# Second layers of seven experts with the token slots stationary, in an attention and expert-routing kernel on one Trainium2 core

## The chip, the cores and the metric

The kernel runs on one core of a Trainium2 chip. The core has engines with instruction streams of their own: TensorE (PE in the profile; its weight loads are listed apart as PEld), VectorE (DVE), ScalarE (ACT), GpSimd (POOL) and SyncE (SP, which here only issues transfers). The metric is the device time of one execution in microseconds (us), lower is better. The kernel before takes 544.92 us (median of 3 runs, 543.99 to 547.03).

## What is computed

Attention over 4 batches, 8 heads, 768 positions, 64 values per head, in which a query sees the first 8 keys and the last 96; the result, 3072 tokens of 512 values, goes into a layer of 8 experts. Each token goes to one expert, the one with the largest gate logit. All arrays are fp32.

```python
def _moe_ref(x, w_gate, w1, w2):          # x: (3072, 512), w1: (8, 512, 1024), w2: (8, 1024, 512)
    logits = x @ w_gate
    expert_idx = np.argmax(logits, axis=1)
    # gate_w: the softmax of logits at expert_idx; tokens sorted by expert (...)
    for e in range(E):
        lo, hi = (boundaries[e], boundaries[e + 1])
        h = np.maximum(x_sorted[lo:hi] @ w1[e], 0.0)
        y_sorted[lo:hi] = h @ w2[e]
    y = y_sorted[inv_perm]
    return gate_w[:, None] * y
```

## The kernel before

The kernel runs attention in units of (batch, pair of heads, third of the sequence), 48 in all. For each unit TensorE makes scores, ScalarE takes exponentials, VectorE multiplies them with the mask and bias, and TensorE multiplies with the values (`attend`). Every second unit is turned (`turn`) so that the gate logits can be made while attention goes on. Finished tokens are stored in `x_tok` in device memory, and an expert's tokens are gathered from there by GpSimd with indices that earlier steps have sorted. Two blocks of expert 0's tokens are looked up and worked on before attention is over; the rest of expert 0 comes as p = 0 in the loop below, with 208 slots.

The experts have fixed numbers of slots, and expert 2 and later are taken in order of their counts:

```python
CAPS = (464, 416, 416, 400, 400, 368, 368, 272)
ORDER = (0, 1, 2, 3, 4, 7, 5, 6)          # so p = 1..7 have 416, 416, 400, 400, 272, 368, 368 slots
NQ = 4
# P = 128, DM = 512, KC = 4, FC = 8, TB = 4, NJ = 4, E = 8
```

The end of attention. `n0` counts units in steps of two, and `nu` is 48:

```python
                for n in two:
                    ...
                    scores(n)
                    ...
                if n0 == nu - 4:
                    fetch_0(0)        # pw = sel x mw on TensorE, rows on VectorE, 8 gathers on GpSimd
                    count_0()         # c2 on TensorE, early on VectorE
                if n0 >= 4:
                    turn(n0 - 4)      # px: four transposes on TensorE, copied by ScalarE
                    for n in two:
                        attend(n - 2)
                ...
                if b == B - 1 and m == 6:
                    half_0(0)         # n0 = 42: makes mw, the operand of pw, on VectorE
    ...
            attend(nu - 2)
            turn_x(xe_0, xq_0[0], TB)                     # VectorE turns gathered rows
            turn(nu - 4)
            attend(nu - 1)
            turn_x(xe_0[:, :, P:2 * P], xq_0[1], TB)
            work(1)                                       # a piece of expert 0's layers on TensorE
            turn(nu - 2)
            expert_w1(w1_1, slice(1, 2))
            work(1)
            logits(B - 1)
            ...
            rows_of(ps_m, "_s", NR * NQ, st.pop(("w", 2)), rows_s)
            identify()
            sort_acc(1, gslot_s)
            fit()
            work(3)
            ...
```

`pw`, `c2`, `px`, `pq` (the logits) and the tables share two PSUM buffers (tag "m").

An expert, cut to what TensorE does and what follows it:

```python
            def sort(p, part, parts):             # VectorE turns part of expert p's gathered rows into xe
                ...
            def hidden(p, between=None):          # first layer: slots move, w1 is stationary
                C = slots(p)
                w1t, xe = ws[p % 2][0], xes.pop(p)
                hT = hp.tile([P, FC, CM], F32, tag="hT", name=f"hT_{p}")
                hTs[p] = hT
                for fc in range(FC):
                    ph = ps_h.tile([P, 512], F32, tag="ph", name=f"ph_{p}_{fc}")
                    for kc in range(KC):
                        nc.tensor.matmul(ph[:, 0:C], lhsT=w1t[:, 0, kc, P * fc:P * fc + P], rhs=xe[:, kc, 0:C],
                                         start=(kc == 0), stop=(kc == KC - 1))
                    done = nc.scalar.activation(hT[:, fc, 0:C], ph[:, 0:C], AF.Relu)
                    if fc < 2 and between:
                        between(2 * fc, 2 * fc + 2)      # the turn of the expert before: two blocks each
                    pace(1 if fc < FC - 1 else len(pending), done)   # gathers of a later expert, held back until done

            def result(p):                        # second layer: slots move, w2 is stationary
                ...
                yT = hp.tile([P, KC, CM], F32, tag="yT", name=f"yT_{p}")
                def turn(q0, q1):                 # back to rows of tokens, 128 at a time
                    for q in range(q0, min(q1, (C + P - 1) // P)):
                        ...
                        for dc in range(KC):
                            nc.tensor.transpose(pt[0:rows, P * dc:P * dc + P], yT[:, dc, o:o + rows], ident)
                        finish(p, q, rows, pt)    # times the gate on VectorE, then a scatter to the output
                cuts = [0, C] if p < E - 1 else [0, (C - 1) // P * P, C]
                for g in range(len(cuts) - 1):
                    c0, c1 = cuts[g:g + 2]
                    for dc in range(KC):
                        po = ps_o.tile([P, DM], F32, tag="po", name=f"po_{p}_{g}_{dc}")
                        for fc in range(FC):
                            nc.tensor.matmul(po[:, 0:c1 - c0], lhsT=w2t[:, 0, fc, P * dc:P * dc + P], rhs=hT[:, fc, c0:c1],
                                             start=(fc == 0), stop=(fc == FC - 1))
                        pace(2 if dc == 0 else 1, nc.vector.tensor_copy(out=yT[:, dc, c0:c1], in_=po[:, 0:c1 - c0]))
                        if p > 0 and 0 < dc < KC - 1:
                            sort(p + 1, dc - 1, KC - 2)
                        ...
                return turn

            for p in range(1, E):
                hidden(p, turn)
                fetch(p + 2, 0)                   # w1 of the expert after next
                plan(p + 2)                       # its gathers
                turn = result(p)
                fetch(p + 2, 1)                   # its w2
```

The early blocks of expert 0 and the gate logits already have the two forms that matter below: `result_0` keeps 128 slots of `hT_0` stationary and moves 512 columns of `w2_0` (`po`, line 340), and `logits` keeps 32 columns of `wg_sb` stationary and writes four groups of 32 partitions (`pq`, line 559).

## Time and profile before

| | |
|---|---|
| time, median of 3 runs | 544.92 us (543.99 to 547.03) |
| span of the profiled execution | 525.5 us |
| granted TensorE clock, mean | 0.993 |
| TensorE's first instruction | at 4.7 us |
| part of the experts' loop (from 197.5 us on) | 328.0 us, TensorE busy 319.9 |
| last TensorE instruction ends | at 517.4 us |

The profile comes from one execution. In it an engine's busy time is the time covered by its instructions, and the chain that ended last is followed back from the last instruction, at each step to what released it or to the instruction before it on its engine. An L and a number name a line of the kernel; `out<-in` are the tensors written and read; a matmul in fp32 shows as two rows. Rows of TensorE overlap[...], so its pace is read from starts, or from the chain, and not from the duration of one.

### The profile page before, as it was taken

What the parts mean: (1) busy time and instruction counts of PE and PEld (TensorE: products, weight loads), DVE (VectorE), ACT (ScalarE), POOL (GpSimd) and SP (SyncE); (2) the same over time, 40 slices, a digit from 0 to 9 for tenths busy, and PEclk for the clock granted to TensorE, in tenths of its full rate; (3) what the DMA queues carried; (4) which work ended last, traced back from release to release, by engine and by line L of the source; (5) the groups of instructions that cost most, each with busy time, mean ns of one, the idle gap of its engine ahead of it and who ended that gap; (6) DMA issues with size and microseconds to landing.
All of it is one profiled execution on the core that took longest, in us unless ns stands there. A gap on an engine that the chain in (4) does not pass through costs nothing.

```text
span 525.5 us, 7951 instructions
## 1 busy us (share of the span) xinstructions
PE 506.7 (96%) x3076; PEld 380.6 (72%) x3076; DVE 197.2 (38%) x506; ACT 126.5 (24%) x227; POOL 136.7 (26%) x161
## 2 busy tenths in 40 slices
PE   4999999999979999999999999999999999999993
PEld 3999999999979949855555556556556886666793
DVE  5877897896954534110320122022012031022011
ACT  4766655654632102011001001101100101101100
POOL 5000000000041276342344226334222735202002
PEclk9999999999989999999999999999999999999998
DMA  9999999899936922954461816456083686001001
GB/s 155 157 155 163 235 164 179 224 164 176 276 113 183 277 54 84 212 181 95 100 217 49 173 40 222 91 107 230 16 175 98 175 172 222 20 1 57 1 2 61
DMA packets 145184, 71.95 MB, mean 137 GB/s; under 512 B 126656, under 2 KB 126660, under 8 KB 145136
## 3 DMA queue, kind: packets, MB, share of 16 engines
q1 hardware_dynamic: 137344, 58.16, 49.0%
q0 software_dynamic: 5264, 12.59, 8.0%
q10 hardware_dynamic: 2528, 0.59, 0.6%
q8 instruction: 26, 0.43, 0.3%
q14 instruction: 22, 0.18, 0.1%
HBM read 59.00 MB, written 12.65 MB: 136 GB/s over the span
## 4 chain that ended last, share of the span: by engine, by line
PE 94%; DVE 2%; POOL 1%; DMA 1%; issue 0%; SPq 0%; ACT 0%; POOLq 0%
PE po L1089 29%; PE ph L1046 29%; PE o L528 14%; PE s L493 8%; PE px L545 3%; PE po L340 3%; PE ph L333 2%; PE pt L1079 2%; PE pq L559 1%; DMA x_tok<-xr 1%; PE pi L618 1%; PE first L428 1%; DVE e L506 0%; DVE kT L429 0%; DVE w_second L510 0%
## 5 line engine op out<-in xcount | busy, mean ns | idle before, releaser
L273 POOL DMA_INDIRECT xq_s<-x_tok,rows_s x72 | 72.6, 1009 | 133.4 <-DVE yT L1091 58.9
L1091 DVE COPY yT<-po 128x416 f32<-128x416 f32 (+6 forms) x36 | 17.6, 488 | 229.4 <-PE po L1089 229.4
L1048 ACT ACTIVATE hT<-ph 128x416 f32<-128x416 f32 (+4 forms) x64 | 29.9, 468 | 281.4 <-PE ph L1046 281.4
L1089 PE MATMUL po<-hT,w_second 128*128 128x416 f32 (+4 forms) x320 | 80.4, 411 | 0.0
L1046 PE MATMUL ph<-xe,w_second 128*128 128x416 f32 (+3 forms) x256 | 80.2, 469 | 0.0
L1046 PE MATMUL ph<-xe,w_first 128*128 128x208 f32 (+3 forms) x256 | 76.5, 456 | 0.0
L1089 PE MATMUL po<-hT,w_first 128*128 128x208 f32 (+3 forms) x256 | 75.5, 456 | 0.0
L1089 PEld LDWEIGHTS po<-hT,w_second 128*128 128x128 f32 x320 | 56.1, 190 | 23.9 <-issue 10.2
L1046 PEld LDWEIGHTS ph<-xe,w_second 128*128 128x128 f32 x256 | 48.0, 190 | 28.1 <-issue 9.9
L1089 PEld LDWEIGHTS po<-hT,w_first 128*128 128x128 f32 x256 | 47.7, 190 | 27.1 <-issue 10.2
L1046 PEld LDWEIGHTS ph<-xe,w_first 128*128 128x128 f32 x256 | 47.3, 190 | 25.8 <-issue 10.0
L273 POOL DMA_INDIRECT xq<-x_tok,rows x15 | 15.3, 1023 | 165.8 <-DVE early L645 142.0
L528 PE MATMUL o<-vt,e 128*128 128x128 f32 x288 | 53.9, 278 | 0.0
L528 PE MATMUL o<-va,e 128*128 128x128 f32 x240 | 46.9, 277 | 0.0
L528 PEld LDWEIGHTS o<-vt,e 128*128 128x128 f32 x288 | 43.2, 195 | 0.2 <-issue 0.2
L493 PE MATMUL s<-qT,kT 64*128 64x128 f32 x384 | 38.7, 286 | 0.9 <-ACT qT L430 0.9
L314 POOL DMA_INDIRECT out_dram<-y,idx_s x21 | 20.5, 976 | 71.8 <-DVE y L322 68.8
L499 ACT ACTIVATE e<-s 128x1024 f32<-128x1024 f32 (+1 forms) x36 | 33.0, 943 | 18.2 <-PE s L493 18.2
L528 PEld LDWEIGHTS o<-va,e 128*128 128x128 f32 x240 | 36.9, 194 | 0.1
L493 PE MATMUL s<-qT,kA 64*128 64x128 f32 x320 | 34.2, 292 | 2.0 <-ACT kA L414 2.0
L493 PEld LDWEIGHTS s<-qT,kT 64*128 64x128 f32 x384 | 30.2, 196 | 2.2 <-ACT qT L430 1.3
L510 DVE TENSOR_TENSOR e<-e,Wb 128x1024 f32<-128x1024 f32 x24 | 28.8, 1213 | 7.4 <-ACT e L499 7.3
(170 smaller groups left out, 491.9 us busy)
## 6 DMA issues: line engine op xcount, KB each, us to landing
w_second<-in_moe_w_dram SPq DMA_DIRECT2D x16, 512.0 KB, 8.6
w_second<-in_moe_w_dram SPq DMA_DIRECT2D x4, 2048.0 KB, 9.1
x_tok<-xr SPq DMA_DIRECT2D x24, 256.0 KB, 3.8
w_first<-in_moe_w_dram SPq DMA_DIRECT2D x12, 512.0 KB, 8.6
w_first<-in_moe_w_dram SPq DMA_DIRECT2D x3, 2048.0 KB, 9.2
vt<-in_v_dram SPq DMA_DIRECT2D x31, 192.0 KB, 3.8
w_second<-in_q_dram SPq DMA_DIRECT2D x60, 96.0 KB, 3.6
w_second<-in_k_dram SPq DMA_DIRECT2D x60, 96.0 KB, 2.9
```

What stands on the lines that cost most here:

```text
L273: return nc.gpsimd.indirect_dma_start(out=xq[:, i, :], out_offset=None, in_=x_tok[0:NJ * top, :], in_offset=bass.IndirectOffsetOnAxis(ap=c ...
L314: p = nc.gpsimd.indirect_dma_start(out=out[:, :], out_offset=bass.IndirectOffsetOnAxis(ap=where, axis=0), in_=y[0:rows, :], in_offset=None ...
L340: nc.tensor.matmul(po, lhsT=hT_0[q][:, fc, :], rhs=w2_0[:, 0, fc, :], start=(fc == 0), stop=(fc == FC - 1))
L493: nc.tensor.matmul(ps[:, h, P * m:P * m + P], lhsT=lhsT, rhs=qT[r, P * i:P * i + P], start=True, stop=True)
L499: nc.scalar.activation(e[:, :, 0:w], ps[:, :, 0:w], AF.Exp, scale=D ** -0.5)
L510: nc.vector.tensor_tensor(out=eh, in0=eh, in1=W[:, 2 * j:2 * j + 2, P:3 * P].rearrange("p h (o c) -> p h o c", o=1).to_broadcast([P, 2, 2, ...
L528: nc.tensor.matmul(po[:, t, h, :], lhsT=pt[:, h, P * m:P * m + P], rhs=(vt if own else va)[:, c0:c0 + P], start=(m == mine[0][0]), stop=(m ...
L545: nc.tensor.transpose(px[:, 2 * i + t, :], xrs[b, c][:, t, P * j:P * j + P], ident)
L1046: nc.tensor.matmul(ph[:, 0:C], lhsT=w1t[:, 0, kc, P * fc:P * fc + P], rhs=xe[:, kc, 0:C], start=(kc == 0), stop=(kc == KC - 1))
L1048: done = nc.scalar.activation(hT[:, fc, 0:C], ph[:, 0:C], AF.Relu)
L1089: nc.tensor.matmul(po[:, 0:c1 - c0], lhsT=w2t[:, 0, fc, P * dc:P * dc + P], rhs=hT[:, fc, c0:c1], start=(fc == 0), stop=(fc == FC - 1))
L1091: pace(2 if dc == 0 else 1, nc.vector.tensor_copy(out=yT[:, dc, c0:c1], in_=po[:, 0:c1 - c0]))
```

## The change

For p = 1 to 7 the second layer is turned round: 128 slots of `hT` are stationary and the 512 columns of `w2` move, so that the result stands in rows of tokens and need not be transposed. What is left beyond full blocks, where it is at most 96 slots, is done in pieces of 32 slots: four column groups of TensorE each take the same 32 slots and 128 columns of `w2`, and the result lies as 128 partitions of (group, slot) x 128 values, which a scatter puts into the output seen as rows of 128. A longer rest (112) is one more block. To scale such a piece the gates are needed in its layout, which `gates_of` makes for all pieces once. A last partial piece is padded with zeros in `hT`. Expert 0 keeps the old form (`along_row`). `hT` has two buffers. The next expert's rows are turned behind the first two blocks. Apart from that, the look-up for expert 0's first blocks moves behind the first `attend` of its step, and `count_0` behind a piece of expert 0's work.

```diff
+    gpc_0 = consts.tile([P, LOTS[1] * TB], F32)
+    gpc_s = consts.tile([P, NR * NQ * TB], F32)
@@
+    def gates_of(pool, ps, nm, ns, gs, to):
+
+        mg = pool.tile([P, NS, TB], F32, tag="mw", name="mg" + nm, bufs=1)[:, 0:ns, :]
+        nc.vector.tensor_tensor(out=mg, in0=gs.rearrange("p (s o) -> p s o", o=1).to_broadcast([P, ns, TB]),
+                                in1=grp.rearrange("p (o g) -> p o g", o=1).to_broadcast([P, ns, TB]), op=ALU.mult)
+        pg = ps.tile([P, NS * TB], F32, tag="m", name="pg" + nm)[:, 0:TB * ns]
+        nc.tensor.matmul(pg, lhsT=sel, rhs=mg.rearrange("p s g -> p (s g)"), start=True, stop=True)
+        nc.vector.tensor_copy(out=to, in_=pg)
@@ (put() takes the view of the output that it writes; scaled() returns its instruction)
+    out_j = out.rearrange("n (j d) -> (n j) d", j=NJ)
@@
-                if n0 == nu - 4:
-                    fetch_0(0)
-                    count_0()
                 if n0 >= 4:
                     turn(n0 - 4)
                     for n in two:
                         attend(n - 2)
+                        if n == nu - 4:
+                            fetch_0(0)
@@
             work(1)
+            count_0()
             turn(nu - 2)
@@
             sort_acc(1, gslot_s)
+            work(1)
+            gates_of(gp, ps_m, "_s", NR * NQ, gslot_s.rearrange("p r q -> p (r q)"), gpc_s)
+            gates_of(gp, ps_m, "_1", LOTS[1], gslot_0[1], gpc_0)
             fit()
-            work(3)
+            work(2)
@@
-            hp = ectx.enter_context(tc.tile_pool(name="hp", bufs=1))
+            hp = ectx.enter_context(tc.tile_pool(name="hp", bufs=2))
@@ (in hidden)
+                if C % 32 > 0:
+                    nc.vector.memset(hT[:, :, C:C // 32 * 32 + 32], 0.0)
@@
+            def finish_piece(p, i, pt):
+
+                r = ORDER[p] - 2
+                c = 2 * TB * p + i if p < 2 else NQ * TB * r + i
+                g, rw = (gpc_0, rows_0[1]) if p < 2 else (gpc_s, rows_s)
+                y = yp.tile([P, DM], F32, tag="y", name=f"y_{p}_p{i}")[:, 0:P]
+                nc.vector.tensor_scalar(out=y, in0=pt, scalar1=g[:, c:c + 1], scalar2=None, op0=ALU.mult)
+                put(y, P, rw[:, c:c + 1], out_j)
@@ (along_row(p, C, w2t, hT) is the old second layer and its turn, without sort() and cuts)
+            def result(p):
+
+                C = slots(p)
+                w2t, hT = ws[p % 2][1], hTs.pop(p)
+                if p == 0:
+                    return along_row(p, C, w2t, hT)
+                rest = C % P if C % P <= 3 * 32 else 0
+                nq = (C - rest + P - 1) // P
+                for q in range(nq):
+                    rows = min(P, C - P * q)
+                    po = ps_o.tile([P, DM], F32, tag="po", name=f"po_{p}_{q}")
+                    for fc in range(FC):
+                        nc.tensor.matmul(po[0:rows, :], lhsT=hT[:, fc, P * q:P * q + rows], rhs=w2t[:, 0, fc, :],
+                                         start=(fc == 0), stop=(fc == FC - 1))
+                    pace(2, finish(p, q, rows, po))
+                    if q < 2:
+                        sort(p + 1, q, 2)
+                for i in range(TB * nq, pieces_of(C) if rest else 0):
+                    pt = ps_t.tile([P, P], F32, tag="pt", name=f"pt_{p}_{i}")
+                    for fc in range(FC):
+                        for g in range(TB):
+                            nc.tensor.matmul(pt[32 * g:32 * g + 32, :], lhsT=hT[:, fc, 32 * i:32 * i + 32],
+                                             rhs=w2t[:, 0, fc, P * g:P * g + P], start=(fc == 0), stop=(fc == FC - 1))
+                    finish_piece(p, i, pt)
```

## The prediction

> **What bounds the kernel.** I read the page first, then the chain that ended last in order of time, then the stretch around 146 us where that chain leaves TensorE. The page's busy times and the chain's shares by engine:
>
> ```profile
> PE 506.7 (96%) x3076; PEld 380.6 (72%) x3076; DVE 197.2 (38%) x506; ACT 126.5 (24%) x227; POOL 136.7 (26%) x161
> ...
> PE 94%; DVE 2%; POOL 1%; DMA 1%; issue 0%; SPq 0%; ACT 0%; POOLq 0%
> ```
>
> TensorE is on the chain for 94% of the span, so a microsecond taken from TensorE's own work is a microsecond off the end, unless another engine then comes late. From the chain in order of time (start, us, what), one stretch of expert 0's early work, one of the gate logits, and then one whole expert of 416 slots with the next one's start:
>
> ```profile
> 168.65 1.48 PE pq L559 x32
> ...
> 185.62 12.05 PE po L340 x28
> ...
> 243.62 22.35 PE po L1089 x64
> 265.97 2.79 PE ph L1046 x8
> 268.76 0.87 PE pt L1079 x8
> 269.63 2.80 PE ph L1046 x8
> 272.43 0.87 PE pt L1079 x8
> ...
> 494.96 15.59 PE po L1089 x80
> ```
>
> Each fp32 matmul is two rows here (8 fc x 4 dc = 32 matmuls, 64 rows); a transpose is one row. What to see: (a) the second layer with 416 slots moving costs 22.35/64 = 349 ns a row; (b) a block's four transposes cost 0.87/2 = 0.437 us, 109 ns each, on the chain between the next expert's first layers; (c) with 512 columns moving and 128 slots stationary (po L340, the form the change uses) a row costs 12.05/28 = 430 ns; (d) with 32 stationary columns and outputs on four partition groups (pq L559) 32 rows of 192 columns take 1.48 us, 46 ns a row. The same chain gives 335.8 ns for 400 slots (21.49/64), 309.2 for 368 (19.79/64), 229.2 for 272 (14.67/64).
>
> Then the timeline around the one long pause of TensorE, and busy time by stretch (us, PE, PEld, DVE, ACT, POOL busy, granted clock, DMA share, GB/s):
>
> ```profile
> 147.61 0.36 PE L268 MATMUL pw<-mw,sel 128*128 128x8 f32 x2 [1.29 <-DVE gslot L633]
> 147.82 0.37 PE L644 MATMUL c<-C_b,ones 128*128 128x8 f32 x2
> 149.80 1.11 PE L545 MATMUL px<-ident,xr 128*128 128x128 f32 x4 [1.61 <-DVE early L645]
> ```
>
> ```profile
> 146.20:149.80 3.60, 0.70 (x8) 0.53 (x5) 3.46 (x12) 1.22 (x2) 0.00 (x0) 0.92 0.45 164
> 149.80:154.90 5.10, 5.10 (x34) 4.98 (x34) 0.61 (x3) 1.85 (x3) 3.95 (x4) 0.72 0.16 38
> ```
>
> TensorE waits for the look-up matmul `pw`, whose operand VectorE makes at the back of its queue, and then for a PSUM buffer: `pw`, `c2` and the transposes `px` share two, and both are held until VectorE has gone through two mask multiplications (1.22 and 0.95 us) and written rows and early. Afterwards the granted clock is 0.72 for 5 us.
>
> [...] In `pq` four rows start 6 to 7 ns apart and the next four 162.5 ns after them[...]. [...] From the place where the row before `pq` would have had its successor (168.49 us) to the first row after it (170.02) are 1.53 us, against 8 rounds x 162.5 = 1.30[...]. [...] Here pauses of 1.29 and 1.61 us with four rows between them were enough for the 0.72.
>
> **The change, part by part.**
>
> Second layers, experts p = 1 to 7. A full block of 128 slots costs 8 fc x 2 rows x 430 = 6.88 us, and a rest of 112 rows as much, since the 512 columns move either way. A piece of 32 slots is 8 fc x 4 groups x 2 = 64 rows in 16 rounds. A round of 128 columns I take at 110 ns (between the 109 of the transposes and the 112 that 128-column matmuls with new weights show), so 16 x 0.110 + 0.23 = 1.99 us. The transposes of `yT` go, 0.437 us a block. Before against after:
>
> 416 slots (p = 1, 2): 22.35 + 4 x 0.437 = 24.10 for the 16 transposes; after 3 x 6.88 + 1.99 = 22.63. Gain 1.47 each, 2.9 together.
> 400 slots (p = 3, 4): 21.49 + 1.75 = 23.24 against 22.63 (rest 16, one piece, padded with zeros). Gain 0.6 each, 1.2 together.
> 272 slots (p = 5): 14.67 + 3 x 0.437 = 15.98 against 2 x 6.88 + 1.99 = 15.75. Gain 0.2.
> 368 slots (p = 6): 19.79 + 1.31 = 21.10 against 3 x 6.88 = 20.64. Gain 0.5.
> 368 slots (p = 7): from 494.96 to the end of the last transposes at 517.45 is 22.49, which contains its own waits for VectorE's copies; against 20.64. Gain 1.8.
>
> Sum 6.6 us.
>
> Expert 0 keeps its old form (208 slots), so nothing moves there.
>
> Look-up moved. Before, TensorE goes from the end of the scores at 146.22 to the next scores at 154.86 in 8.64 us, and the work in it is 0.59 (px) + 3.13 (28 rows of o) + 0.2 (pw) = 3.92; `c2` goes elsewhere. After, `px` finds a free buffer at once, the first `attend` has its operands (its mask multiplication ended at 144.5), and by the time `pw` comes, at about 148.2, its operand (147.47) is there. So the pause and the slow clock go: 8.64 - 3.92 = 4.7, less 0.2 for `c2` later: 4.5 us. The gathers start at about 150.5, as late as before (VectorE still has the two multiplications ahead), while the work that uses them comes 4.6 us earlier: four gathers at 1.31 us each plus 2.6 to landing end at about 157, and the rows are turned at 158.6 behind `attend`; TensorE asks for them at 159.8. The other four land at 162.5 to 163.5, and their rows are wanted several pieces of work later. But `early` stands behind their turning on VectorE and holds the buffer that the last gate logits need at 164.3: up to 0.4 us, 0.2 counted.
>
> Added: two `gates_of`, whose products pass DVE, PE, DVE, PE in turn. VectorE has the gates of the late experts about 1.9 us after `pw_s`, TensorE one piece of work of 1.72, so 0.25 of waiting; the second must wait for the first's copy and a multiplication (0.25 + 0.2, and some hand-over), 0.6; the four rows 0.35. Sum 1.2 us lost.
>
> Next rows transposed behind the first two blocks: VectorE's 216 ns a piece (18.4/85) is small. Only expert 5, of two blocks, is close: 6 pieces after its second block (13.76 + 0.2 + 0.75 + 1.3 = 16.0) against TensorE done at 15.75: 0.3 lost. For the others the rows are ready at about 16.2 of 22.5 us. The second buffer of `hT` frees nothing that TensorE waits for today.
>
> Sum: -6.6 - 4.5 + 0.2 + 1.2 + 0.3 = -9.4 us, of which the pause is nearly half. The span would go from 525.5 to 516.1, and the time, which lies 19.4 above the profiled span, from 544.9 to 535.5.
>
> **Rivals.** First, the pieces do not overlap: 64 x 0.110 = 7.0 us each instead of 1.99, five of them, 25 us more, 560 us. Against it stands `pq`, the same form of loop with the same split over groups. A milder form, in which weight loads set the pace at 46 ns a row as in `pq`, makes 3.1 a piece and costs 5.5 us: 541. [...] Second, the pause only moves: the gathers, as late as before, hold up expert 0's early work. With a landing 2 us later, 2 of the 4.5 would be lost: 537.5. Third, the next expert's rows come late, since gathers now go two behind each block and one behind each activation. The last is issued at the end of the first layer and lands about 4 us into the second, while the first turning comes at 6.9, so I see no wait. Fourth, the new zero padding of `hT` for expert 0 stands on VectorE behind the turning of expert 1's rows, which waits for gathers until about 203 us; if the activations of expert 0 had to follow it, some 7 us would go (543). They write other columns, and in the trace TensorE reads one half of `xe_0` at 164.47 while the turning of the other half, interleaved with it, comes at 165.24, so waits go by what is really written. Weights: DMA is at a share of 0.48 over a 416-slot expert and 0.72 over the shortest, so a slightly shorter expert doesn't make it the bound.
>
> **Range.** What I am surest of is the pause, then the 430 and 349 ns. The loosest terms are the piece (1.8 to 3.1, five times) and small waits at the ends of blocks, which can only cost: TensorE's idle time apart from this pause lies at the start and in the tail, and the change touches neither. The times before spread by 3 us. I give 535.5 us, 532 to 540. Faster by 2% means under 534.0, which needs 10.9 us: chances 0.30 faster, 0.68 same, 0.02 slower.
>
> **What would show it.** 16 rows a block at 430 ns and no `pt` transposes after expert 0; a piece of 64 rows in about 2 us; no pause and no clock under 0.9 between 146 and 155; about 1 us of TensorE waiting at the two gate products; the next first layer starting without a wait, but for expert 6. It is wrong if pieces take over 3 us, or if TensorE waits for `xe` at any expert's start.

## The result, and the profile after

| | before | after |
|---|---|---|
| time, median (range), 4 runs each | 544.68 us (543.99 to 547.03) | 531.63 us (529.59 to 531.98) |
| ratio after/before | | 0.9745, 95% interval 0.9707 to 0.9784 |
| profiled execution: span, and its own time | 525.5 us, 527.35 us | 529.5 us, 531.48 us |

The medians differ by 13.05 us; the ratio says 2.55%. The prediction was 535.5 us, 532 to 540: the result lies 3.9 us under its middle and just outside the range. The last row of the table is the first surprise. The profile of after has a *longer* span than that of before, although its time is 13 us shorter; and in each of the two profiled executions the time is only 2 us above the span, not 19.4. The profile before is of an execution that took 527 us, one that the 544 to 547 us of the timed runs don't resemble.

The page of after, its busy times and its chain's shares by engine:

```profile
PE 503.4 (95%) x3108; PEld 348.2 (66%) x3108; DVE 181.3 (34%) x484; ACT 126.7 (24%) x227; POOL 138.5 (26%) x161
...
PE 82%; another core or an unknown queue 5%; SPq 5%; DVE 3%; DMA 2%; ACT 1%; issue 1%; POOL 0%; POOLq 0%; ACTq 0%; DVEq 0%
```

TensorE is busy 3.3 us less, and VectorE 15.9. But TensorE's share of the chain fell from 94% to 82%: something new holds it. The chain in order of time (start, us, what) first shows the part that was changed on purpose:

```profile
275.08 22.54 PE ph L1065 x64
297.62 20.60 PE po L1119 x48
318.22 1.89 PE pt L1128 x64
...
423.32 13.75 PE po L1119 x32
...
437.76 1.28 DVE xe L295 x6
...
439.08 20.05 PE ph L1065 x64
```

`po L1119` is the new second layer: three blocks of 16 rows in 20.60 us, 429 ns a row from start to start (on the page a row's record is 592 ns long: the records overlap). `pt L1128` is a piece of 32 slots: its 64 rows take 1.89 us. The transposes of `yT` between the next expert's first layers are gone. Ahead of expert 6 (at 439.08) the chain goes through VectorE's turning of its rows; that is the one place where the loop waits.

The busy times by stretch (span, length in us, then PE, PEld, DVE, ACT, POOL, granted clock, DMA share, GB/s), in the same two windows as before:

```profile
146.20:149.80 3.60, 3.55 (x39) 3.15 (x37) 3.43 (x13) 3.21 (x5) 0.00 (x0) 1.00 0.08 30
149.80:154.90 5.10, 5.10 (x61) 4.86 (x60) 3.02 (x7) 1.92 (x3) 2.85 (x3) 1.00 0.11 29
```

TensorE is busy 3.55 of 3.60 us where it was busy 0.70, and the clock stays at 1.00 where it was 0.72. The pause is gone.

To see where the rest went I cut each trace at the first instructions of TensorE's stages. Here "first before" is the profile of before that the prediction used, and "e1" another execution of the same kernel, from the experiments below, whose time (548.5 us) is near those of the timed runs (544 to 547):

| TensorE's stretch, us | first before | e1 (before again) | after |
|---|---|---|---|
| A: first row to the scores of the last two units | 150.14 | 152.48 | 146.69 |
| B: to expert 0's early first layer | 9.62 | 15.05 | 9.96 |
| C: early first layer, with the last logits | 19.07 | 19.06 | 19.24 |
| D: early second layer, in after with the two gate products | 13.96 | 16.32 | 16.41 |
| E: expert 0's late first layer | 11.25 | 20.91 | 20.76 |
| F: its second layer | 11.25 | 11.25 | 11.25 |
| G: experts 1 to 7, to the last row of TensorE | 297.44 | 297.71 | 291.13 |
| H: from there to the end | 8.04 | 7.94 | 9.40 |
| span | 525.5 | 546.6 | 529.5 |

(The first row starts at 4.7, 5.9 and 4.7 us.) Stretch G is what was predicted. B, D and E are not: the usual execution of before loses 5.4 us in B and 12 us in D and E that the first profile didn't have. After doesn't lose the 5.4, but D and E are as long in it as in e1.

What this loss looks like is seen in the timeline of after, 186 to 208 us (start, us, engine, what, and in brackets the idle time before and what ended it):

```profile
193.04 0.75 DVE L335 TENSOR_SCALAR y<-po,gslot 128x512 f32<-128x512 f32 x1 [3.75 <-remote]
...
202.88 0.34 PE L1065 MATMUL ph<-xe,w_first 128*128 128x208 f32 x1 [1.06 <-issue]
...
207.14 0.75 DVE L335 TENSOR_SCALAR y<-po,gslot 128x512 f32<-128x512 f32 x1 [11.97 <-remote]
207.35 0.81 ACT L1067 ACTIVATE hT<-ph 128x208 f32<-128x208 f32 x3 [26.07 <-remote]
207.75 9.44 PE L1065 MATMUL ph<-xe,w_first 128*128 128x208 f32 x36 [4.53 <-ACT hT L1067]
```

VectorE scales the second early block (207.14) 10 us after that block's last row on TensorE ended (197.13 by the trace). ScalarE takes up the first column block of the late first layer at 207.35, though its rows ended at 198.54. TensorE, out of PSUM buffers, waits for ScalarE. They had been idle for 11.97 and 26.07 us by then: the trace's record of TensorE's semaphore has no update between 193.02 and 207.11 us, and then four within 0.3 us (207.11, 207.21, 207.30, 207.39). The signals "this matmul is done" arrived up to 10 us late. The stops are 0.48, 1.06 and 4.53 us, and after the last the granted clock is 0.5 for 6.83 us, which costs half of that: 11.25 + 6.07 + 3.4 = 20.7 for stretch E, measured 20.76. TensorE's own rows don't show it: for the last row of the second early block the recorded end is 197.13 and the update 207.11. For comparison, in the experts' loop of the same trace VectorE takes up each block of 128 slots 0.04 us after its recorded end.

Two limits of this reading. The trace holds these two times, 10 us apart, and nothing that says which of them is the end of the matmul, so it can't tell a late signal from a matmul that itself ended late; "late signal" stands for both below. And of the three stops only the last, 4.53 us, waits for another engine. Those of 0.48 and 1.06 us stand in the middle of a column block and carry `issue`: TensorE waits there for nothing that the profile shows. So TensorE itself is held up too, and not only those that wait for it.

Throughout this time, from 177.4 to 203.1 us, GpSimd issues 20 indirect gathers, one after the other with 0.30 us between them (7 for expert 0's late slots, 13 for expert 1). That made the suspicion for the experiments.

### The profile page after: what moved, and what is told of

Its sections match the earlier page's. It is cut to its first block, busy times and chain, and to the rows that moved or that the text cites. A ratio compares the mean times of both kernels' runs of the same rounds, so it can differ in the third digit from the quotient of the medians.

```text
span 529.5 us, 7971 instructions
## 1 busy us (share of the span) xinstructions
PE 503.4 (95%) x3108; PEld 348.2 (66%) x3108; DVE 181.3 (34%) x484; ACT 126.7 (24%) x227; POOL 138.5 (26%) x161
## 4 chain that ended last, share of the span: by engine, by line
PE 82%; another core or an unknown queue 5%; SPq 5%; DVE 3%; DMA 2%; ACT 1%; issue 1%; POOL 0%; POOLq 0%; ACTq 0%; DVEq 0%
PE ph L1065 29%; PE po L1119 26%; PE o L542 11%; PE s L507 5%; SPq L409 4%; PE ph L347 2%; PE po L1102 2%; PE px L559 2%; PE pt L1128 1%; PE pq L573 1%; PE pi L632 1%; DMA vt<-in_v_dram 1%; DMA x_tok<-xr 1%; DMA k_first<-in_k_dram 1%
## 5 line engine op out<-in xcount | busy, mean ns | idle before, releaser
L1065 PE MATMUL ph<-xe,w_first 128*128 128x208 f32 (+3 forms) x256 | 79.3, 471 | 6.2 <-ACT hT L1067 4.5
L335 DVE TENSOR_SCALAR y<-po,gslot_s 128x512 f32<-128x512 f32 (+1 forms) x17 | 12.8, 751 | 201.5 <-PE po L1119 201.5
L1119 PE MATMUL po<-w_second,hT 128*128 128x512 f32 (+1 forms) x176 | 76.2, 592 | 0.0
L1065 PEld LDWEIGHTS ph<-xe,w_first 128*128 128x128 f32 x256 | 50.2, 200 | 34.4 <-issue 11.4
L1119 PE MATMUL po<-w_first,hT 128*128 128x512 f32 (+1 forms) x144 | 62.3, 592 | 0.0
L1119 PEld LDWEIGHTS po<-w_second,hT 128*128 128x128 f32 (+1 forms) x176 | 33.2, 189 | 41.3 <-issue 40.7
L327 POOL DMA_INDIRECT out_dram<-y,idx_s x17 | 17.2, 1011 | 124.7 <-DVE xe L295 71.7
L1119 PEld LDWEIGHTS po<-w_first,hT 128*128 128x128 f32 (+1 forms) x144 | 27.2, 189 | 34.0 <-issue 33.5
```

What stands on the lines that cost most here:

```text
L327: p = nc.gpsimd.indirect_dma_start(out=to[:, :], out_offset=bass.IndirectOffsetOnAxis(ap=where, axis=0), in_=y[0:rows, :], in_offset=None, ...
L335: done = nc.vector.tensor_scalar(out=y[0:rows, :], in0=po[0:rows, :], scalar1=gs[0:rows, :], scalar2=None, op0=ALU.mult)
L1119: nc.tensor.matmul(po[0:rows, :], lhsT=hT[:, fc, P * q:P * q + rows], rhs=w2t[:, 0, fc, :], start=(fc == 0), stop=(fc == FC - 1))
```

## The experiments

Theory: a long unbroken series of gathers on GpSimd delays TensorE's signals, and what waits for them then stops TensorE; the change gained more than predicted because it took the first such series (8 gathers for expert 0's first blocks) out of reach of a wait. Rivals: the second layers gained more than their count; the pause itself was longer than it looked; the gate products or the new zero padding stop TensorE; the first profile was merely a lucky execution.

The kernels were run in five groups. Those of a group share one chip and the runs of the kernel before there, and the groups turned out to differ: on chips A, C, D and E before took 546.2, 546.4, 549.3 and 546.0 us, on chip B 529.5 (527.2 to 531.4). No group holds both kinds. Each chip was seen in one group only, so that it is the chip which makes the difference, and not the hour, is likely but not shown.

### Chip A: which part of the change gives what

**The kernel before once more**, unchanged.

> The kernel before, unchanged, once more with a profile. The first profile of it has a span of 525.5 us, while its timed runs are at 544, and a span is only about 2 us below its time (529.5 against 531.5 for the changed kernel), so the first profile isn't typical by some 17 us. Theory A: after a pause TensorE really works at about half its pace for a long time, longer in the typical run than in that profile, so that this run shows a span near 542 us, with the extra 17 us after the pause at 146 us, and waiters released microseconds after the recorded end of the matmul that they wait for. Rival B: the extra time is spread over the experts' loop (transposes, moving slots), and the stretch from 146 to 200 us looks as in the first profile. Time near 544.7 either way.

Measured: 546.88 us, ratio to the other runs of before 1.0006 (0.9985 to 1.0027), span 546.6. So time and span do not differ by 19 us: they differ by 2, and it was the first profile that was of an execution 17 us shorter than the timed runs. Rival B is out: G is 297.71 against 297.44. Theory A is right about the place, but the extra time is not a slow pace that starts with the pause: C is as short as in the first profile, and E, long after the pause, loses the most. The timeline of this execution where it loses stretch B's 5.4 us:

```profile
150.88 0.36 PE L268 MATMUL pw<-mw,sel 128*128 128x8 f32 x2 [1.30 <-DVE gslot L633]
...
153.06 0.66 PE L545 MATMUL px<-ident,xr 128*128 128x128 f32 x4 [1.60 <-DVE rows L269]
...
163.42 0.50 PE L528 MATMUL o<-vt,e 128*128 128x128 f32 x3 [0.70 <-issue]
164.16 0.27 PE L528 MATMUL o<-vt,e 128*128 128x128 f32 x1 [0.24 <-issue]
164.90 0.36 PE L528 MATMUL o<-vt,e 128*128 128x128 f32 x1 [0.47 <-issue]
...
167.96 0.77 PE L528 MATMUL o<-va,e 128*128 128x128 f32 x2 [1.80 <-DVE recips L532]
```

The two waits at 150.88 and 153.06 are the pause that the prediction knew, 1.30 and 1.60 us. The stops from 163.42 on are new. The first three come at the end of the series of 8 gathers (153.3 to 163.6 us), and the granted clock is 0.5 for 3.41 us from 167.5 on. ScalarE had begun the exponentials of a score block at 161.99, 2.4 us after its last row (159.57).

**The change without the moved look-up.**

```diff
+                if n0 == nu - 4:
+                    fetch_0(0)
+                    count_0()
                 if n0 >= 4:
                     turn(n0 - 4)
                     for n in two:
                         attend(n - 2)
-                        if n == nu - 4:
-                            fetch_0(0)
@@
             work(1)
-            count_0()
```

> The changed kernel with expert 0's look-up and count back in their old places (the pause at 146 us is there again); everything else is kept. Theory A: it loses the 4.5 us of the pause and, if the slow time after that pause is what costs the kernel before 17 us, up to that as well: 536 to 550 us. Rival B: the pause and its slow clock cost 4.5 us as in the first profile, so 536.

Measured: 540.40 us, ratio 0.9893 (0.9861 to 0.9926): 5.8 us gained, within theory A's wide range and 4 over rival B's 536. Stretch G is 291.23, B 13.67.

**The kernel before with the moved look-up alone** (the same lines the other way round).

> The kernel before with the look-up and the count moved, and nothing else. Theory A: the pause goes, and with it the slow time that costs the typical run 17 us more than the first profile: 544.7 - 4.5 - up to 17, so 523 to 535 us. Rival B: 544.7 - 4.5 = 540 us.

Measured: 537.64 us, ratio 0.9837 (0.9807 to 0.9866): 8.6 us gained, where the prediction gave this part 4.5 less 0.2. It lies between theory A (523 to 535) and rival B (540). Stretch G is unchanged at 297.71, A 145.45, B 10.72; D and E are 37.4 together, as long as in e1 (37.2). The two parts add up: 5.8 + 8.6 = 14.4, against the 13 to 13.8 of the whole on the chips with late signals. So the second layers did not exceed their count, and the surplus sits in the look-up's part. B fell by 4.3 against e1, and this is the bulk of it. A fell by 7.0 in this pair of profiles, but A varies by 2 us between executions of one kernel: it is 151.4 on average over the five profiles with the old look-up (150.1 to 152.5) and 146.4 over the fifteen with the new one (145.5 to 147.6), so 5.0 less, close to the predicted 4.5. E also shows that neither the gate products nor the zero padding make the loss there: this kernel has neither, and its E is 23.16.

**The gate products without their pauses**: both products on VectorE first, two pieces of work, then both matmuls and their copies.

```diff
             sort_acc(1, gslot_s)
-            work(1)
-            gates_of(gp, ps_m, "_s", ...)
-            gates_of(gp, ps_m, "_1", ...)
-            fit()
+            mg_s = gates_times(gp, "_s", ...)
+            mg_1 = gates_times(gp, "_1", ...)
             work(2)
+            gates_of(ps_m, "_s", NR * NQ, mg_s, gpc_s)
+            gates_of(ps_m, "_1", LOTS[1], mg_1, gpc_0)
+            fit()
+            work(1)
```

> The changed kernel with both products of the gates made by VectorE ahead and both matmuls behind two pieces of work instead of one, so that TensorE doesn't wait for VectorE between them. In the profile of the changed kernel TensorE pauses there for 1.4 us at 185 us, and then waiters are released later and later, up to 10 us after the recorded end of the last matmul of expert 0's early block. Theory A (the pause starts a slow stretch): the pause and the stretch go, 531.6 - 1.4 - about 8 to 10 = 520 to 522 us. Rival B (the late release has another cause, as the weights' or instruction transfers at that time): only the pause goes, 530 us.

Measured: 532.68 us, ratio 0.9752 (0.9721 to 0.9782): neither theory A's 520 to 522 nor rival B's 530. D is 15.64, but E 20.35: D and E together are 36.0 against 37.2 in after. A pause of 1.39 us ahead of the second product (in after) was saved on TensorE's side and for the most part given back a few microseconds later.

### Chip B: a chip without late signals

**Expert 1's gathers spread** (one behind each of the last four pieces of work, one behind each activation of expert 0).

```diff
-            work(4)
+            plan(1)
+            work(4, 1)                 # a gather behind each piece
@@
-        take(1)
@@ (in along_row)
+                    if 0 < dc < KC - 1:
+                        sort(1, dc - 1, KC - 2)
@@ (ahead of hidden(0))
-            sort(1, 0, 1)
```

> The changed kernel with expert 1's 13 gathers, which now follow each other in one burst with the 7 before them (177 to 204 us), put one behind each of the last four pieces of expert 0's early second layer and one behind each activation of expert 0's late first layer; the turning of expert 1's rows moves into expert 0's late second layer. Theory C: while GpSimd issues gathers without a break, TensorE's semaphore updates reach the waiting engines up to 10 us late (rows of matmuls begin on time, their ends are signalled late), and TensorE then stops for want of a free PSUM buffer. Then fewer gathers in a row mean less delay, and of the 12 us that the stretch from expert 0's early second layer to the end of its late first layer takes over its 25.2 us of work (37.2 in the changed kernel), 5 to 10 go: 522 to 527 us. Rival D: the delay has to do with TensorE's own rows or clock there, and the gathers only happen to run then: 531 us.

Measured: 524.18 us, ratio 0.9890 (0.9850 to 0.9930). The number lies in theory C's range only because this chip loses nothing anyway: E is 11.25 here, but also in the next run, where nothing is spread. Spreading cost time instead: the first layer of expert 1 waits 1.92 us for its rows, and the experts' loop is 3.8 us longer than in the next run.

**All gathers of a later expert in one burst**, behind the first block.

```diff
-                    pace(2, finish(p, q, rows, po))
+                    pace(len(pending), finish(p, q, rows, po))
```

> The changed kernel with all 12 or 13 gathers for an expert issued in one burst behind the first block of a second layer, instead of two behind each block and one behind each activation. Theory C: the late signals appear in the experts' loop too, where there are none now; a burst of 17 us reaches from the second block into the next first layer, and holds up the turning of rows and the activations: 2 to 10 us for each of five experts, 540 to 580 us. Rival D: 531 us, no change.

Measured: 520.19 us, ratio 0.9819 (0.9780 to 0.9858). Neither theory C's 540 to 580 nor rival D's 531 came true. No harm anywhere: A 146.44, B 9.62, D 15.52, E 11.25, G 291.14.

**The change without the gathers of expert 1** (its rows are left out; the time is that of the rest).

```diff
-        take(1)
+        plan(1)
+        del pending[:]
```

> The changed kernel without the 13 gathers of expert 1 (this leaves expert 1's rows out: zeros take their place, all else is done as before). Theory C: the burst ends at 186 us instead of 204, and the stretch from expert 0's early second layer to the end of its late first layer falls from 37.2 us to 26 to 29: 521 to 525 us. Rival D: 531 us.

Measured: 519.26 us, ratio 0.9807 (0.9767 to 0.9847), the same within 1 us as with a burst everywhere.

**The kernel before without the gathers of expert 0's first two blocks** (256 of its slots are left out):

```diff
-                    gather(xq_0[h], rows_0[i][:, TB * h:TB * h + TB], min(n, TB), N - S if i == 0 else N)
+                    if i > 0:
+                        gather(xq_0[h], rows_0[i][:, TB * h:TB * h + TB], min(n, TB), N)
```

> The kernel before without the 8 gathers of expert 0's first two blocks (this leaves the rows of those 256 slots out; zeros take their place). The typical run of it needs 15.0 us from the scores of unit 46 to expert 0's early work, against 9.6 of work, and has TensorE stopped for 0.2 to 1.8 us four times there. Theory C: those stops are late signals from the burst of 8 gathers, and go: 546 - 4 to 6 = 540 to 542 us; the pause before it stays. Rival A (a slow TensorE after the pause): the stretch stays at 14 to 15 us, 546.

Measured: 531.40 us, ratio 1.0030 (1.0016 to 1.0044). Taking gathers away gains nothing on this chip, because nothing was lost to them: B is 9.62, D 13.96 and E 11.25 with and without, as in the first profile of before, whose 527.35 us is also of this kind. So this group says nothing about the theory. It shows that the first profile was no single accident: all 23 runs of before here are of its kind.

### Chip C: the same questions where signals are late

**The changed kernel again.**

> The changed kernel, unchanged. The kernel before took 546.2 us on one chip (late signals from TensorE in the gather bursts) and 529.5 on another (none, as in the first profile of it, whose span was 525.5). On a chip without late signals the sum of the prediction should hold as it stands: 529.5 - 9.4 = 520 us. On one with them 531.6 again.

Measured: 533.42 us, ratio 0.9737 (0.9700 to 0.9774). D and E together are 38.8.

**Without the gathers of expert 1** (rows left out, as on chip B).

> The changed kernel without the 13 gathers of expert 1 (its rows are left out, zeros take their place), once more, because the chip of its first run showed no late signals. On a chip with late signals, theory C (unbroken gathers delay them): 521 to 525 us, the stretch from expert 0's early second layer to the end of its late first layer at 26 to 30 us instead of 37.2. Theory D (they have nothing to do with gathers): 531. On a chip without late signals: 519, as before.

Measured: 520.56 us, ratio 0.9521 (0.9483 to 0.9559): 12.9 us less than the changed kernel beside it, where the same edit did nothing on chip B. Its timeline in stretch E:

```profile
197.33 11.42 PE L1066 MATMUL ph<-xe,w_first 128*128 128x208 f32 x64
197.53 0.75 DVE L335 TENSOR_SCALAR y<-po,gslot 128x512 f32<-128x512 f32 x1 [4.74 <-PE po L354]
...
199.06 0.34 ACT L1068 ACTIVATE hT<-ph 128x208 f32<-128x208 f32 x1 [17.48 <-PE ph L1066]
```

All 64 rows run through without a stop; VectorE and ScalarE are released by TensorE at once, not by something "remote" ten microseconds later. Here the turning of expert 1's rows on VectorE stands where it stands in the changed kernel.

**All gathers of a later expert in one burst.**

> The changed kernel with each later expert's 12 or 13 gathers in one burst behind the first block, once more for the same reason. On a chip with late signals, theory C: they appear in the experts' loop, 540 to 580 us; theory D: 531. Without late signals: 520, as before.

Measured: 579.83 us, ratio 1.0589 (1.0550 to 1.0628): 46 us *slower* than the changed kernel beside it, and at the upper end of theory C's range. The same kernel took 520.19 on chip B. TensorE in the same piece of 32 slots, first on chip B, then on chip C:

```profile
263.39 1.95 PE L1128 MATMUL pt<-w_second,hT 128*32 128x128 f32 x64
265.42 0.35 DVE L1083 TENSOR_SCALAR y_p<-pt,gpc 128x128 f32<-128x128 f32 x1 [1.17 <-PE pt L1128]
```

```profile
273.56 1.39 PE L1128 MATMUL pt<-w_second,hT 128*32 128x128 f32 x41
273.67 0.75 DVE L335 TENSOR_SCALAR y<-po,gslot 128x512 f32<-128x512 f32 x1 [4.74 <-PE po L1119]
275.27 0.30 PE L1128 MATMUL pt<-w_second,hT 128*32 128x128 f32 x2 [0.33 <-issue]
275.98 0.29 PE L1128 MATMUL pt<-w_second,hT 128*32 128x128 f32 x1 [0.41 <-issue]
277.39 0.38 PE L1128 MATMUL pt<-w_second,hT 128*32 128x128 f32 x3 [1.11 <-issue]
```

On chip C the gathers of this burst run from 262.3 to 279.0 us. The last full block ends in the middle of them and VectorE takes it up at 273.67, still 0.04 us after its recorded end. The stops begin 1.4 us into the piece, whose rows are short: 64 in 1.9 us, against 16 in 6.87 us for a block. All 35 stops of 0.15 us and more that the loop's pieces show carry `issue`, 23.3 us together; outside the pieces there is one, 0.6 us. Stretch G is 340.9 us against 291.1. Behind the stops come 41.0 us at half clock, which cost up to 20.5; the remaining 5 or so were not traced.

The same 28 us by stretch, counted from 1.0 us after the start of the burst's scatter, on chip B and then on chip C (columns as above):

```profile
251.83:279.83 28.00, 28.00 (x134) 14.54 (x133) 3.23 (x10) 2.35 (x5) 16.00 (x16) 1.00 0.49 151
```

```profile
262.00:290.00 28.00, 21.96 (x104) 10.54 (x103) 3.23 (x10) 0.52 (x1) 16.03 (x16) 0.88 0.36 110
```

GpSimd issues the same 16 transfers in both. The DMA engines are busier on chip B, where nothing is stopped (0.49 against 0.36, 151 GB/s against 110), so it is not the amount of data that crowds anything out. On chip C TensorE is stopped for 6 of 28 us and its clock is 0.88.

The changed kernel has the same pieces, with groups of three transfers, and its loop loses no time. Yet signals are late in it as well, on such a chip. In after:

```profile
273.13 1.96 PE L1128 MATMUL pt<-w_second,hT 128*32 128x128 f32 x64
277.79 0.35 DVE L1083 TENSOR_SCALAR y_p<-pt,gpc 128x128 f32<-128x128 f32 x1 [3.80 <-remote]
```

VectorE takes up this piece 2.7 us after its recorded end, and the other four 2.7 to 3.4 us after theirs; in the first pair above, on chip B, it is 0.07. Nobody waits for a piece, so this costs nothing. In the first 146 us of the same trace, before the gathers, no signal of TensorE that another engine waited for came more than 0.07 us late, though the gate logits put 32 rows into 1.44 us there.

**The gate products without their pauses**, here beside the changed kernel.

> The changed kernel with both products of the gates behind two pieces of work instead of one. On a chip without late signals TensorE stopped 0.5 us between the two products in kernels of this form, and the wait before the first was 0.2: 520 - 0.7 = 519.5 us. With late signals 532 to 533 as in its first run, no gain.

Measured: 531.58 us, ratio 0.9716 (0.9675 to 0.9757), which overlaps with the changed kernel's 0.9737 (0.9700 to 0.9774). What the gate products cost on such a chip is not resolved: 1.8 us between the medians here, and 1.05 the other way between e4 and the first runs of after.

### Chip D: the first series, fewer signals, shorter groups

**The kernel before without the gathers of expert 0's first two blocks** (256 slots left out).

> The kernel before without the 8 gathers of expert 0's first two blocks (the rows of those 256 slots are left out, zeros take their place), once more, because the chip of its first run showed no late signals. On a chip with late signals, theory C: the stretch from the scores of unit 46 to expert 0's early work falls from 15.0 us to 9.6 to 10, so 546 - 5 = 541 us, and the pause at 146 us stays. If instead the slow clock after the pause is what costs there, 545 to 546. On a chip without late signals: 530, as before.

Measured: 542.31 us, ratio 0.9885 (0.9835 to 0.9936). B falls to 9.62, its work, from 15.05 in e1, while the pause at 146 us keeps its two waits (1.28 and 1.60 us). So the 5.4 us in B come from the 8 gathers, and these are not what makes the pause.

**Half as many signals to wait for**: on top of the gate version, two column blocks of expert 0's late first layer share a PSUM buffer and one activation.

```diff
-                for fc in range(FC):
+                nf = 2 if p == 0 else 1
+                for fc in range(0, FC, nf):
@@
-                    done = nc.scalar.activation(hT[:, fc, 0:C], ph[:, 0:C], AF.Relu)
+                    done = nc.scalar.activation(hT[:, fc:fc + nf, 0:C], ph[:, 0:nf * C].rearrange(...), AF.Relu)
```

> The changed kernel with the products of the gates behind two pieces of work, and with two of expert 0's 208-slot hidden chunks in one PSUM bank and one activation for both, so that TensorE can do six chunks instead of three before it needs a signal back. On a chip with late signals: the stop in expert 0's late first layer begins some 4 us later and is that much shorter, and with it the half clock that follows: 532 - 5 to 8 = 524 to 527 us. On a chip without: 519 to 520, nothing gained by it.

Measured: 529.91 us, ratio 0.9668 (0.9618 to 0.9718): the expected 524 to 527 was missed. D and E are 34.0 together, 3.2 us less than in after and 2.0 and 2.9 less than in the two runs of the gate version (on other chips). By the profile TensorE waits for no other engine in E any more, but it still stops for 4.8 us there (`issue`).

**Four gathers behind each block instead of two.**

> The changed kernel with four gathers behind each block of a second layer instead of two. [...] On a chip with late signals, theory C: bursts of four gathers and a scatter last 6.5 us and end when the next block does, so that what is late is waited for by nobody: 532 to 536 us, between 533.4 (two) and 579.8 (all thirteen). On a chip without: 520.

Measured: 564.35 us, ratio 1.0284 (1.0219 to 1.0349). My expectation missed by some 30 us: G grew from 291 to 324. GpSimd's timeline tells why. With four gathers behind each block and a scatter behind each of those, the three groups of an expert run together: 15 indirect transfers from 261.5 to 281.5 us with no break over 0.6 us, and TensorE's first stop begins at 276.0, 14 us into them. With pairs, as in the changed kernel, each group of three transfers ends about 3.2 us before the next begins, and G loses nothing. So this was not a half measure but one more unbroken series. How long the series has run does not set the moment of the first stop, though: in f3 as in e12 it comes 1.3 to 2.0 us after the start of a piece in each of the five experts that have one, at 14 us into the series for the first of them and at 7 for the last, and all stops of the loop but one per run lie in pieces. In the loop of e1, where no rows are shorter than the transposes' 109 ns and those come by the eight, four series of 8 to 10 transfers (10 to 13 us) cost nothing: its G is 297.71, on a chip without late signals 297.44.

### Chip E: keep the gathers, break the series

So far gathers had been taken out, or put into longer series; that could still be their number. These versions keep all 13 gathers of expert 1 and spread them: in g1 one behind each of the last six pieces of work (1.72 us apart), one behind every second activation of expert 0, three behind its second layer's copies. The turning of expert 1's rows on VectorE moves behind those copies with them; e11 had shown that E runs through with the turning in its old place. g2 does the like on top of the version with half the signals.

```diff
             fit()
-            work(2)
+            plan(1)
+            work(2, 1)                 # a gather behind each piece
             turn_x(xe_0, xq_0[0], TB)
             turn_x(xe_0[:, :, P:2 * P], xq_0[1], pieces_of(C0) - TB)
-            work(4)
+            work(4, 1)
@@
-        take(1)
@@ (ahead of hidden(0); in along_row sort(1, ...) comes in two parts, as in e5)
-            sort(1, 0, 1)
@@ (in hidden)
-                    pace(1 if fc < FC - 1 else len(pending), done)
+                    pace(len(pending) if fc == FC - 1 and p > 0 else 1 if p > 0 or fc % 2 == 0 else 0, done)
```

> The changed kernel with expert 1's 13 gathers taken out of the unbroken series: one behind each of the last six pieces of expert 0's early second layer (1.72 us apart), one behind every second activation of its late first layer (2.8 us apart), the last three behind its second layer's copies. Theory (an unbroken series of gathers delays TensorE's signals, on the chips where it does so at all): expert 0's late first layer falls from about 20 us to near its work of 11.25, so 522 to 525 us where the kernel before takes 544 to 549; 521 to 523 where that takes 530. Rival (the number of gathers counts, not their being unbroken): expert 0's part stays at some 36 to 37 us from the start of the early second layer to the end of the late first one, 530 to 534 us.

> The same spreading on top of the version with both gates' products behind two pieces of work and two column blocks per PSUM buffer in expert 0's late first layer (half as many signals to wait for): one gather behind each of the last five pieces of work, one behind each of the four activations, four behind the second layer's copies. Theory: 520 to 524 us where the kernel before takes 544 to 549. Rival: 528 to 531, as that version without the spreading (529.9).

> The changed kernel itself on this chip, for the comparison with the two spread versions: 530 to 534 us if the kernel before takes 544 to 549 (signals late), 520 to 523 if that takes about 530 (none late).

Measured: g1 526.56 us, ratio 0.9635 (0.9576 to 0.9695); g2 **524.70 us, 0.9606 (0.9549 to 0.9664)**; the changed kernel beside them 532.18 us, 0.9737 (0.9681 to 0.9792). Stretch E is 11.25 in both, its work, against 21.75 beside them: the loss is gone with every gather still there. The spreading is not complete even so: from 197.5 to 203.8 us in g1 three gathers and two scatters follow each other without a break, beside E, and TensorE does not stop. The timeline of g1 where E begins, and where it gives part of it back:

```profile
197.08 11.42 PE L1068 MATMUL ph<-xe,w_first 128*128 128x208 f32 x64
208.33 11.42 PE L1105 MATMUL po<-hT,w_first 128*128 128x208 f32 x64
...
223.40 4.75 PE L1068 MATMUL ph<-xe,w_second 128*128 128x416 f32 x8 [3.53 <-DVE xe L295]
```

Expert 1's last rows now land late: its first layer waits 3.53 us for VectorE's turning of them, and runs its first 8 rows in 4.75 us where 2.90 is usual, 5.4 us in all. That is why the expected 522 to 525 was missed by 1.6 us in g1; g2 is 0.7 over its 520 to 524, and waits 3.69 us at the same place. Version g2 beats both kernels: 21.3 us under before, 7.5 under the changed one. Spreading that lets the rows land some 4 us sooner would be the next step; it was not tried.

## Why the prediction was wrong

**The second layers: right.** Predicted −6.6 and +0.3 for expert 6; stretch G went from 297.71 to 291.23 and 291.28 on chip A, −6.4 to −6.5. Rows 429 ns (430), blocks 6.87 us (6.88; for p = 6, whose third block has 112 slots, the three took 20.60 us as well), a piece 1.89 (1.99). Expert 6 came late by 0.27 (20.05 in its first layer on the chain against the 19.79 of the same form), predicted 0.3. The first rival, pieces that do not overlap, needed 7.0 us a piece and is out, and so is its milder form with 3.1.

**The pause: right in kind and about in size.** Stretch A fell by 3.5 us against the first profile and by 5.8 against e1, predicted 4.5 (it varies by 2 us between executions of one kernel; the averages above differ by 5.0). The second rival, a pause that only moves, is out: B is 9.96 to 9.99 in the three profiles of after, against 9.62 in the first profile of before.

**The gate products: about right.** On the chip without late signals D is 15.52 against 13.96, 1.6 for a predicted 1.2. With late signals the pause ahead of the second is 1.39 us, but D and E together are no longer than before.

**Third and fourth rival: neither.** No expert's rows came late in the changed kernel beyond expert 6 (p = 6). TensorE does stop in E, where the fourth rival put a stop of 7 us, but the zero padding is not the cause: e6, on chip B, has the same padding at the same place in VectorE's queue and no stop, and e1 and e3 lose as much in E without it.

**The step that failed** is this one: "The span would go from 525.5 to 516.1, and the time, which lies 19.4 above the profiled span, from 544.9 to 535.5." The 19.4 us were taken for a fixed difference between two ways of measuring one thing. They are the difference between two kinds of execution, one with the stops beside the gathers and one without, and in the five groups the kind went with the chip: time and span of one execution differ by 2 us in every run here. So the prediction summed the gain of a kernel that did not have the trouble, and subtracted it from the time of one that did. On its own kind of chip the sum holds: 529.5 to 520.2 us on chip B (e6, the changed kernel but for its pacing; its G is 291.14, that of the changed kernel 291.13), −9.3 for a predicted −9.4 (so close by luck in part: A alone varies by 2 us between executions). On the others two terms were missing. The look-up's part, "4.5 us" less 0.2, gained 8.6 alone (e3), and this is the term that carried the result out of the range: the old place of it put a series of 8 gathers beside scores and exponentials that needed TensorE's signals (f1: B falls by 5.4 without those gathers). And a loss of 10 us (after) to 12 us (before) in D and E stayed in both kernels, which the first profile could not show, so "TensorE's idle time apart from this pause lies at the start and in the tail" was untrue of the kernel that was timed. H, 1.4 us longer in after than in before, took a little back. It is 9.1 to 9.4 in nine of the profiles and 6.7 to 8.2 in the others, with the old loop in both sets (e9 and f1 have 9.1 and 9.4), so it does not belong to the change; what lengthens it was not looked into.

The warning stood in the open. A time 19 us above the profiled span, 3.7%, was more than the whole expected gain, and the runs spread by only 3 us. It asked for a second reading: either the profile is of another kind of execution, or part of the time is out of its sight. The prediction chose neither and carried the number along.

**What stays open.** That unbroken series of gathers delay TensorE's signals on chips A, C, D and E is shown by taking them out (e11, f1), adding to them (e12, f3) and spreading them (g1, g2). What carries the delay is not. The amount of data is out (chip B moves more without harm). The stops have a rhythm of their own: in E of e1 TensorE starts again at 213.61, 215.01, 216.41 and 217.81 us, 1.40 apart, and in the piece of e12 in steps of 0.7 or 1.4, while the gathers come every 1.30. Whether the recording of the trace has a part in it is open. Some records are missing: in after, 420 updates of VectorE's semaphore are on record for 448 instructions that make one, and 14 to 42 are missing in every profile of chips A, C, D and E, while on chip B and in the first profile of before the two counts agree within 2. But they are missing as well in e11 and g2, where E lost nothing, and in every run here the trace was recorded; none without stands beside them. Nor is it shown why the series of 8 gathers does little in its new place: in after it runs from 151.4 to 162.6 us, beside all of B, whose work is the same, and the signals there are late by no more than 1.6 us; its third and fourth gather took 1.63 and 1.21 us instead of 1.00.

## What to carry to other kernels

Compare the span of a profiled execution with the timed runs before reading anything else; here they differ by 2 us in one and the same execution, so 19 meant that the profile was of another case than the one that was timed. When an engine waits long for a matmul whose recorded end is past, look at what the signal shares its time with: here a series of indirect gathers on GpSimd, which needs no wait in common with TensorE to stop it. Where signals were late, indirect gathers were better issued singly or in pairs behind the work of another engine than in one series beside short rows (chip C: 533.42 us with pairs, 579.83 with bursts; chip E: 526.56 spread, 532.18 with the series), as long as the last of them still landed before it was needed; on chip B spreading them only cost time (524.18 us, against 520.19 with bursts).

## What the hardware did that I had not expected

- On four of five chips signals of TensorE arrived up to 10 us late while GpSimd issued gathers in an unbroken series (1.00 us each, 0.30 between): 10 to 12 us lost with 20 in a row, 46 us when every expert's gathers were one burst, 31 us (against another chip) with 15 gathers and scatters running together, nothing with groups of three and 3.2 us between them or with single gathers 1.72 us apart. A series of 7 (178.4 to 187.3 us in g1) left no mark: D is 15.46 there, 15.52 on chip B.
- In the loop it is the short rows that suffer: the stops begin 1.3 to 2.0 us into a piece of 64 rows in 1.9 us, after up to 13 us of the series beside blocks of 16 rows in 6.87 us whose signals are 0.04 us late. (The rows in E take 176 ns each, those of a block 429.) Why is not shown.
- It seems to depend on the chip: on one of five the kernel with bursts took 520 us, on another 580.
- The late signal is counted twice. In stretch E of after the stops of 6.1 us were followed by 6.83 us of clock at 0.5, another 3.4 us.
- Four groups of 32 columns gave 64 fp32 rows of 128 columns in 1.89 us, 0.1 less than 16 rounds of the transposes' 109 ns with 0.23 us, the excess of 1.53 us over 1.30 that the prediction had read around the logits' rows; what makes that excess is not shown.
